# Logit rounds over pairs of head groups, split turns of the first x chunks, and finer tracking of output stores in an attention and gated-MLP block

## The chip, the core and the metric

The kernel runs on one core of a Trainium2 chip. A core has five engines that each follow their own list of instructions and meet at semaphores: TensorE (PE) for matmuls, VectorE (DVE), ScalarE (ACT), GpSimd (POOL) and SyncE (SP), which here issues every DMA. PE writes to PSUM, eight banks of 2 KB per partition; the other engines read it from there. SBUF has 128 partitions.

The metric is the device time of one execution in microseconds. Before: a median of 805.42 over three runs (805.29 to 806.07).

## The reference

Two layers over x of 2048 rows by 1024 columns, bf16. Heads: 32 of width 32; the rows are cut into 4 segments of 512.

```python
h  = x + A(layernorm(x))
h2 = h + B(layernorm(h))

# A, per head and segment s (M, z start at 0)
p     = softmax(q k^T * scale + causal mask)
a_dot = p @ v
a_mem = (phi(q) @ M) / (phi(q) @ z + 1e-6)        # phi(t) = t + 1 if t > 0 else exp(t)
o     = g * a_mem + (1 - g) * a_dot               # g = sigmoid(beta), one per head
M    += phi(k)^T v ;  z += sum(phi(k))
out   = o @ wo

# B
z1, z2 = split(gelu(x @ w_in));  z2 = layernorm(z2)
out    = (z1 * (w_sp @ z2 + b_sp)) @ w_out
```

## The kernel before

**A planner in the kernel.** Helpers (`mm`, `act`, `copy`, `tt`, `dma` and so on) only record operations, each with what it reads and writes and an estimated cost. `_Prog.op` (L91) finds the dependencies: SBUF in pieces of 32 bytes, PSUM by bank, DRAM outputs by `_where` (L78) in blocks of 128 rows. `schedule` (L148) then simulates the engines. PE keeps the order in which its operations were recorded; ACT, DVE, POOL and SP take, at each moment, the ready operation of lowest priority number, which is the recording index plus `prio`. The resulting order per engine is fixed in the program, and `link` adds the semaphore waits. So an edit of the recording order can change the order on every engine, and an engine waits at an instruction whose operands are late even if a later one could run.

**Start.** Fourteen matmuls on zeros warm up PE. `x_load` brings four chunks of 128 rows of x into XIN, halves of the weights follow on the same queue. `layernorm` takes statistics on DVE, the inverse deviation on POOL and the scaling on DVE. For segment 0, `x_turn_pe` (L548) transposes a chunk on PE, 8 transposes into one PSUM bank, and copies it to XNT (chunk 0: half by DVE and then half by ACT; chunks 1 to 3: ACT alone). Later chunks are transposed by DMA (`x_turn`). Chunk tcl+1 is turned on PE ahead of the V product of chunk tcl. Then Pq(0), Pk(0) and phi(0).

**Attention.** A step n covers one head group c = n mod 8 (4 heads) of segment s = n div 8; there are 32. For each:

- `Pq`, `Pk`: 8 matmuls of 128x512 each, copied by ACT (or DVE, for q in segment 0) into QK, which has two buffers.
- `phi`: Exp on ACT, then a minimum and one or two fused operations on DVE; K's phi is transposed by DMA into PK.
- `logits(n, r)` (L609): a round writes the transposed logits of 4 heads into PSUM banks 0 to 3, one head per bank and per row tile (`mm_row`, 32 rows each, the four run side by side). Key block j of 128 keys needs 512 - 128j query columns. Round 0 is j=0 with 512 columns, round 1 is j=1 with 384, round 2 is j=2 and 3 with 256 and 128. An exp on ACT then moves the round to E (two buffers, one for even n, one for odd), and POOL masks the diagonal blocks, one instruction of 128x512 per j. All rounds use the same four banks, so a round waits for the previous exp.
- `X(n)`: the products of E and V for query blocks 0 to 2, 24 matmuls of 33 columns.
- `MZU(n)`: the memory products (from segment 1), the E-V products of query block 3, and the update of M and z (up to segment 2). Then `combine` on DVE and POOL.

The loop over n, at L774, records: logits(n,0); Pq(n+1); X(n-1); logits(n,1); Pk(n+1); MZU(n-1); logits(n,2); phi(n+1); and then the step's fillers, V products of the next heads or segment (`v_group`) and output projections of the segment before (`wo_group`); last come loads and norms for later. Banks 4 to 7 go round for all but the logits.

**The second layer.** From 298.6 us on: w_in products with Gelu (`c1_z2`, `c1_z1`), then for each of four row blocks the w_sp products (`c2`) and the w_out products (`c3`, L935). `c2` adds a row of b_sp (BROW) into TG and multiplies into one of NY = 18 tiles Y. `c3` reads h back from the output tensor, adds, and stores column parts: two of 512 per chunk of rows, and 512, 384 and 128 for the last one. SP waits at the end for every DMA.

Of the kernel before, what the change touches and what calls it, by code (L numbers as in the profile page):

```python
# [35 lines left out]
class _Prog:  # L36
# [41 lines left out]
    def _where(self, ap):  # L78
        n = ap.tensor.name
        if n == self.psum:  # L80
            sz = mybir.dt.size(ap.dtype)
            span = ap.offset + sum(st * (c - 1) for (st, c) in [tuple(x) for x in ap.ap][1:])
            per = 2048 // sz
            off = ap.offset % (8 * per)
            last = off + span - ap.offset
            return "P", tuple(range(off // per, last // per + 1))
        if n in self.base:
            return "S", self._sbuf(ap)
        return "D", ((n, ap.offset // (128 * D)),)

# [237 lines left out]
def bass_sequential_preLN__memory_aug_infini_attn__mixer_gmlp__prompt_kernel(  # L328
# [53 lines left out]
    R_E = region(20480)  # L382
    E = [tens("e%d" % i, [128, 4, 1280], BF16, R_E + i * 10240) for i in range(2)]
    R_OT = region(16384)
# [5 lines left out]
    R_Q = cur[0]  # L390
    QK = [tens("qk%d" % i, [128, 2, L], BF16) for i in range(2)]
    EX = [tens("ex%d" % i, [128, 2, L], BF16) for i in range(1)]
# [17 lines left out]
    STATS = [tens("stats%d" % i, [128, 4, 6], F32) for i in range(4)]  # L410
    MV = [tens("mv%d" % i, [128, 2], F32) for i in range(4)]
    RS = [tens("rs%d" % i, [128, 1], F32) for i in range(4)]
    RA = [tens("ra%d" % i, [128, 12], F32) for i in range(4)]
    RM = [tens("rm%d" % i, [128, 12], F32) for i in range(4)]

    BROW = [tens("brow%d" % i, [128, L], BF16) for i in range(2)]
    TG = [tens("tg%d" % i, [128, L], BF16) for i in range(2)]
    R_END = cur[0]

    N_WARM = 14  # L420
    PS = nc.alloc_psum_tensor("ps", [128, 8, 512], F32)
    G.psum = PS.name

# [21 lines left out]

    def act(o, i, func, scale=1.0, prio=0):
        G.op(ACT, lambda e: e.activation(o, i, func, scale=scale), [i], [o],  # L447
             ((172 if inps(i) else 224) + n_of(i)) / 1.2 + 26, prio=prio, name=str(func))
# [71 lines left out]

    def layernorm(src, dst, w, prio=0):
        late[0] = prio
        k = ln_rr[0] % 4
        ln_rr[0] += 1
        nch = (w + 511) // 512
        cs = w // nch
        for ci in range(nch):
            si, so = src[:, ci * cs:(ci + 1) * cs], STATS[k][:, ci, :]
            G.op(DVE, lambda e, si=si, so=so: e.bn_stats(so, si), [si], [so], (cs + 143) / 0.96, name="bn_stats",  # L529
                 prio=late[0])  # L530
        sa, mv = STATS[k][:, 0:nch, :], MV[k][:]
        G.op(DVE, lambda e: e.bn_aggr(mv, sa), [sa], [mv], 250, name="bn_aggr", prio=late[0])  # L532
        pts1(RS[k][:], MV[k][:, 1:2], LN_EPS, ALU.add)
        ptt(RS[k][:], RS[k][:], MHALF[:], ALU.pow)
        ts(dst, src, MV[k][:, 0:1], RS[k][:], ALU.subtract, ALU.mult)
        late[0] = 0


    OFF = [0, 512, 896, 1152]
    NJ = [512, 384, 256, 128]  # L540

    def x_load(tc):
# [5 lines left out]
    def x_turn_pe(tc):  # L548
        b = bank()
        bb = b.bitcast(BF16)  # L550
        for i in range(8):
            tr(bb[:, i * 128:(i + 1) * 128], XIN[tc][:, i * 128:(i + 1) * 128])
        dst = XNT[0][:, :, tc * 128:(tc + 1) * 128]
        bv = bb.rearrange("p (c n) -> p c n", c=8)
        if tc == 0:
            copy(dst[:, 0:4, :], bv[:, 0:4, :])
            act(dst[:, 4:8, :], bv[:, 4:8, :], ACTF.Copy)
        else:
            act(dst, bv, ACTF.Copy)

# [10 lines left out]
    def Pq(n):  # L571
        s, c = divmod(n, 8)
        b = proj(WQ, s, c)
        if s == 0 and n > 0:
            copy(QK[n % 2][:, 0, :], b)
        else:
            act(QK[n % 2][:, 0, :], b, ACTF.Copy)

    def Pk(n):
        s, c = divmod(n, 8)  # L580
        act(QK[n % 2][:, 1, :], proj(WK, s, c), ACTF.Copy)

    def phi(n):
        s, c = divmod(n, 8)
        lo, hi = (0 if s >= 1 else 1), (2 if s <= 2 else 1)
        q, ex = QK[n % 2], EX[0]
        act(ex[:, lo:hi, :], q[:, lo:hi, :], ACTF.Exp, prio=40)
# [20 lines left out]

    def logits(n, r):  # L609
        q = QK[n % 2]  # L610
        js = (r,) if r < 2 else (2, 3)
        w = NJ[r] if r < 2 else 384
        for j in js:
            o0 = 0 if j < 3 else 256
            for i in range(4):
                p = slice(32 * i, 32 * i + 32)
                mm_row(PS[:, i, o0:o0 + NJ[j]], q[p, 1, j * 128:(j + 1) * 128], q[p, 0, j * 128:512], i, i == 3)
        act(E[n % 2][:, :, OFF[r]:OFF[r] + w], PS[:, 0:4, 0:w], ACTF.Exp, scale=float(SCALE))
        for j in js:
            d = E[n % 2][:, :, OFF[j]:OFF[j] + 128]  # L620
            G.op(POOL, lambda e, d=d: e.affine_select(d, d, [[0, 4], [1, 128]], ALU.is_ge, 0.0, base=0,  # L621
                                                      channel_multiplier=-1), [d], [d], 640, name="mask")

    def pv_mm(n, qb, b, col):
        s, c = divmod(n, 8)
        for i in range(4):
            for j in range(qb + 1):
                o = OFF[j] + (qb - j) * 128
                mm(b[:, col + i * 33:col + (i + 1) * 33], E[n % 2][:, i, o:o + 128], V[s % 2][:, j, 4 * c + i, 0:33],
                   j == 0, j == qb)  # L630
# [94 lines left out]
    for tcl in range(4):  # L725
        layernorm(XIN[tcl][:], XIN[tcl][:], D)
    x_turn_pe(0)
    for tcl in range(4):
        if tcl < 3:
            x_turn_pe(tcl + 1)  # L730
        v_group(0, tcl, 0)
    Pq(0)
    Pk(0)
    phi(0)

# [15 lines left out]
    plan = []  # L751
    for n in range(33):
        s, c = divmod(n, 8)
# [7 lines left out]
        if 1 <= s <= 3:  # L761
            k = (0, 0, 2, 2, 1, 1, 1, 1) if s <= 2 else (0, 0, 1, 0, 1, 1, 2, 3)
            wos = [(s - 1, g) for g in range(sum(k[:c]), sum(k[:c + 1]))]
# [10 lines left out]

    for n in range(32):
        s, c = divmod(n, 8)
        vs, wos = plan[n]
        for a, g in plan[n + 1][1]:
            if g % 2 == 0:
                h_load(4 * a + g // 2)  # L780
        logits(n, 0)
        if n + 1 < 32:
            Pq(n + 1)
        else:
            wo_group(*wos.pop(0))
        if n >= 1:
            X(n - 1)
        logits(n, 1)
        if n + 1 < 32:
            Pk(n + 1)  # L790
        else:
            wo_group(*wos.pop(0))
        if n >= 1:
            MZU(n - 1)
        logits(n, 2)
        if n + 1 < 32:
            phi(n + 1)
        for a in vs:
            v_group(*a)
        for a in wos:  # L800
            wo_group(*a)
        if n < 4:
# [15 lines left out]
        if s == 3:  # L818
# [5 lines left out]
            if c >= 6:  # L824
                win_load(c - 3)


# [76 lines left out]
    WSPT = [WSPT0, tens("wspT1", [128, 16, L], BF16, R_XNT)]  # L904
    spans[:] = [[R + 28672, R_WIN + 57344], [R_M + 2048, R_M_END]]
    NY = 18
    Y = [take("y%d" % i, [128, L], BF16) for i in range(NY)]

# [102 lines left out]
```

## Time and profile before

| what | us |
|---|---|
| median of the runs | 805.42 |
| the profiled execution, as timed | 804.33 |
| its span on the core | 802.6 |
| start, until the first logit round | 22.5 |
| segment 0 | 22.5 to 91.0 |
| segments 1 and 2 | 91.0 to 243.8 |
| segment 3 | 243.8 to 298.6 |
| second layer | 298.6 to 802.6 |
| exp of a round of 512 columns (128x2048), mean | 1.874 |
| exp of a round of 384 columns (128x1536), mean | 1.443 |
| mask of one diagonal (128x512), mean | 0.697 |

The profile is one execution, all engines recorded. Its page gives busy time by engine, the chain of work that ended last, and groups of instructions (line, engine, operation, result and operands, shapes, count; busy time and mean; idle time before it and what ended that). Other views of the same trace show instructions in order of time, or busy time by stage. Matmuls are pipelined: a row of eight starts one every 0.216 us although a single one is listed with 379 ns, so starts and not ends tell when PE was held up. TensorE's granted clock is 1.0 throughout the stages.

The landings of the first loads, from the trace's DMA events: chunk 0 at 2.95 and 3.26 us (two halves), chunk 1 at 4.94, the first half of wv at 7.95, chunk 2 at 8.63, chunk 3 at 9.33, wq at 12.33, wk at 15.35.

### The profile page before, as it was taken

The numbers are of one execution on the slowest core, as the hardware profiler recorded it, in microseconds if no ns is written. First come the engines' busy times: TensorE is split into PE (matmuls) and PEld (weight loads), VectorE is DVE, ScalarE is ACT, GpSimd is POOL, SyncE is SP. The second block draws the span as 40 slices with busy tenths as digits, with TensorE's granted clock in tenths as the row PEclk, the third lists the DMA queues.
The fourth block names the chain that finished last, engine by engine and source line by source line (L and its number), as shares of the span: only waits on it lengthen the run. The fifth ranks groups of instructions, "written<-read, shape, count | busy, mean of one in ns | idle before, by whom it ended". The sixth has DMA issues, their size and how long they took to land.

```text
span 802.6 us, 12722 instructions
## 1 busy us (share of the span) xinstructions
PE 793.7 (99%) x5372; PEld 382.7 (48%) x5372; DVE 368.6 (46%) x846; ACT 299.5 (37%) x344; POOL 154.2 (19%) x321
## 2 busy tenths in 40 slices
PE   7999999999999999999999999999999999999998
PEld 3445455555555555444445454444444444444444
DVE  5783578867766687714215041133223223322322
ACT  3888877787778863133333333100000000000000
POOL 2464445544444341100001010000000000000000
PEclk9999999999999999999999999999999999999999
DMA  9757524534233658520000026803400530011001
GB/s 309 140 129 177 114 67 87 96 84 91 69 48 95 162 107 211 170 66 1 1 1 1 3 55 129 214 1 63 128 27 1 124 93 1 0 63 49 1 7 47
DMA packets 128458, 64.81 MB, mean 81 GB/s; under 512 B 95504, under 2 KB 120336, under 8 KB 128400
## 3 DMA queue, kind: packets, MB, share of 16 engines
q1 hardware_dynamic: 128400, 63.99, 33.2%
q8 instruction: 42, 0.69, 0.4%
q14 instruction: 16, 0.13, 0.1%
HBM read 32.51 MB, written 8.39 MB: 51 GB/s over the span
## 4 chain that ended last, share of the span: by engine, by line
PE 96%; DMA 1%; ACT 1%; DVE 1%; SPq 0%; issue 0%
PE ps L435 93%; PE ps L440 3%; DMA xin<-in_A_x_dram 1%; DVE stats L529 0%; ACT e L447 0%; SPq L490 0%; ACT ex L447 0%; ACT qk L447 0%; PE ps L444 0%; DVE qk L459 0%; DVE xin L463 0%; DVE hx L469 0%; DVE mv L532 0%
## 5 line engine op out<-in xcount | busy, mean ns | idle before, releaser
L435 PE MATMUL ps<-wspT,z 128*128 128x512 bf16 x896 | 194.0, 379 | 0.0
L447 ACT ACTIVATE e<-ps 128x1536 bf16<-128x1536 f32 (+1 forms) x96 | 152.3, 1587 | 38.9 <-PE ps L440 38.9
L435 PEld LDWEIGHTS ps<-wspT,z 128*128 128x128 bf16 x896 | 87.7, 98 | 105.7
L447 ACT ACTIVATE z<-ps 128x512 bf16<-128x512 f32 x120 | 68.2, 569 | 140.0 <-PE ps L435 140.0
L469 DVE TENSOR_TENSOR tg<-ps,brow 128x512 bf16<-128x512 f32 x56 | 38.7, 692 | 152.6 <-PE ps L435 122.7
L621 POOL TENSOR_SCALAR_AFFINE_SELECT e<-e 128x512 bf16<-128x512 bf16 x128 | 88.3, 697 | 98.7 <-ACT e L447 98.4
L435 PE MATMUL ps<-win,hnT 128*128 128x512 bf16 (+1 forms) x512 | 97.8, 352 | 0.0
L435 PE MATMUL ps<-wout,y 128*128 128x512 bf16 (+2 forms) x462 | 97.4, 373 | 0.0
L435 PE MATMUL ps<-hnT,win 128*128 128x512 bf16 x448 | 97.3, 379 | 0.0
L529 DVE BATCH_NORM_STATS2 stats<-z 128x6 f32<-128x448 bf16 x64 | 39.9, 624 | 95.1 <-ACT z L447 93.5
L469 DVE TENSOR_TENSOR hx<-hx,ps 128x512 bf16<-128x512 bf16 (+1 forms) x65 | 43.6, 677 | 79.4 <-PE ps L435 77.0
L435 PEld LDWEIGHTS ps<-win,hnT 128*128 128x128 bf16 x512 | 50.0, 98 | 47.8 <-ACT e L447 0.2
L435 PEld LDWEIGHTS ps<-wout,y 128*128 128x128 bf16 x462 | 44.7, 98 | 52.3
L435 PEld LDWEIGHTS ps<-hnT,win 128*128 128x128 bf16 x448 | 43.9, 98 | 52.1
L435 PE MATMUL ps<-xnT,wk 128*128 128x512 bf16 x256 | 60.8, 380 | 0.0
L435 PE MATMUL ps<-xnT,wq 128*128 128x512 bf16 x256 | 60.8, 380 | 0.0
L435 PE MATMUL ps<-wv,xnT 128*128 128x512 bf16 x256 | 59.9, 380 | 0.1
L435 PE MATMUL ps<-wo,oT 128*128 128x512 bf16 x256 | 58.8, 379 | 0.0
L483 POOL TENSOR_SCALAR rs<-mv 128x1 f32<-128x1 f32 x48 | 10.7, 223 | 185.0 <-DVE mv L532 184.5
L435 PEld LDWEIGHTS ps<-v,e 128*128 128x128 bf16 x1280 | 40.5, 96 | 9.2
L435 PE MATMUL ps<-v,e 128*128 128x33 bf16 x1280 | 42.0, 177 | 0.0
L447 ACT ACTIVATE qk<-ps 128x512 bf16<-128x512 f32 x57 | 34.1, 598 | 10.9 <-PE ps L435 10.4
(58 smaller groups left out, 565.6 us busy)
## 6 DMA issues: line engine op xcount, KB each, us to landing
win<-in_B_w_in_dram SPq DMA_DIRECT2D x6, 1024.0 KB, 5.5
hx<-in_A_x_dram SPq DMA_DIRECT2D x16, 256.0 KB, 3.0
out_dram<-hx SPq DMA_DIRECT2D x16, 256.0 KB, 2.4
hx<-out_dram SPq DMA_DIRECT2D x16, 256.0 KB, 2.6
out_dram<-hx SPq DMA_DIRECT2D x31, 128.0 KB, 1.8
xin<-in_A_x_dram SPq DMA_DIRECT2D x15, 256.0 KB, 6.0
wout<-in_B_w_out_dram SPq DMA_DIRECT2D x2, 1792.0 KB, 10.2
wv<-in_A_wv_dram SPq DMA_DIRECT2D x2, 1024.0 KB, 9.1
```

The costliest lines, as they stand in the source:

```text
L435: G.op(PE, lambda e: e.matmul(o, lhsT, rhs, start=start, stop=stop), [lhsT, rhs], [o], max(n / 2.4 + 2.6, 25.0), lag=166, name="mm " + lhs ...
L440: G.op(PE, lambda e: e.matmul(o, lhsT, rhs, start=True, stop=True, tile_position=(32 * i, 0)), [lhsT, rhs], [o], n / 2.4 if last else 3.5, ...
L447: G.op(ACT, lambda e: e.activation(o, i, func, scale=scale), [i], [o], ((172 if inps(i) else 224) + n_of(i)) / 1.2 + 26, prio=prio, name=s ...
L469: G.op(DVE, lambda e: e.tensor_tensor(o, a, b, op), [a, b], [o], vcost(o, [a, b], fast), name="tt", prio=late[0])
L483: G.op(POOL, lambda e: e.tensor_single_scalar(o, i, s, op), [i], [o], 220 if n_of(o) < 8 else 220 + 2.5 * n_of(o), name="pts1", prio=late[0])
L529: G.op(DVE, lambda e, si=si, so=so: e.bn_stats(so, si), [si], [so], (cs + 143) / 0.96, name="bn_stats", prio=late[0])
L621: G.op(POOL, lambda e, d=d: e.affine_select(d, d, [[0, 4], [1, 128]], ALU.is_ge, 0.0, base=0, channel_multiplier=-1), [d], [d], 640, name= ...
```

## The change

Everything is computed as before; order, buffers and tracking change.

1. **Rounds.** The loop runs over 16 pairs (a, b) of head groups with five rounds of 512 columns: (a, j=0); (a, j=1) with (a, j=3); (a, j=2) with (b, j=2); (b, j=0); (b, j=1) with (b, j=3). E becomes one tensor with a region for each kind of round, and an exp writes the second and third kind in blocks of 256 columns. A mask instruction covers 4 diagonal blocks for j=0 and 8 for the others. QK gets a third buffer, since three groups are alive. The pair's fillers are dealt to five slots.
2. **Start.** A turn uses two banks, 4 transposes each; the first is copied by DVE (ahead of other work, `late` = -200), the second by ACT. The turn of the next chunk stands after five of the eight V matmuls. Pk(0) is made in two parts, K columns 0 to 127 first.
3. **Stores.** A DRAM access is tracked by row block and by 128-column block.
4. **Small.** Y has 14 tiles; BROW and TG move into memory that the first layer leaves; MV is wider; `layernorm` can scale on ACT, which no call uses (`BYACT` is all 0).

```diff
-        return "D", ((n, ap.offset // (128 * D)),)
+        w = list(ap.ap)[-1][1]
+        c0 = ap.offset % D
+        return "D", tuple((n, ap.offset // (128 * D), c) for c in range(c0 // 128, (c0 + w + 127) // 128))
...
-    E = [tens("e%d" % i, [128, 4, 1280], BF16, R_E + i * 10240) for i in range(2)]
+    E = tens("e", [128, 10240], BF16, R_E)
...
-    QK = [tens("qk%d" % i, [128, 2, L], BF16) for i in range(2)]
+    QK = [tens("qk%d" % i, [128, 2, L], BF16) for i in range(3)]
...
+    AT = [5, 5, 5, 9]
...
     def x_turn_pe(tc):
-        b = bank()
-        bb = b.bitcast(BF16)
-        for i in range(8):
-            tr(bb[:, i * 128:(i + 1) * 128], XIN[tc][:, i * 128:(i + 1) * 128])
         dst = XNT[0][:, :, tc * 128:(tc + 1) * 128]
-        bv = bb.rearrange("p (c n) -> p c n", c=8)
-        if tc == 0:
-            copy(dst[:, 0:4, :], bv[:, 0:4, :])
-            act(dst[:, 4:8, :], bv[:, 4:8, :], ACTF.Copy)
-        else:
-            act(dst, bv, ACTF.Copy)
+        for h in range(2):
+            bb = bank().bitcast(BF16)
+            for i in range(4):
+                c = 4 * h + i
+                tr(bb[:, i * 128:(i + 1) * 128], XIN[tc][:, c * 128:(c + 1) * 128])
+            bv = bb[:, 0:512].rearrange("p (c n) -> p c n", c=4)
+            if h == 0:
+                late[0] = -200
+                copy(dst[:, 0:4, :], bv)
+                late[0] = 0
+            else:
+                act(dst[:, 4:8, :], bv, ACTF.Copy)
...
+    def logits(parts):
+        for n, j, col in parts:
+            q = QK[n % 3]
             for i in range(4):
                 p = slice(32 * i, 32 * i + 32)
+                mm_row(PS[:, i, col:col + NJ[j]], q[p, 1, j * 128:(j + 1) * 128], q[p, 0, j * 128:512], i, i == 3)
+        n, j, _ = parts[0]
+        m, src = n % 2, PS[:, 0:4, :]
...
+        elif j == 2:
+            src = PS[:, 0:4, :].rearrange("p i (b q) -> p b i q", b=2)
+            o = E[:, ER3[0]:ER3[0] + 2048].rearrange("p (b i q) -> p b i q", b=2, i=4)
...
+        act(o, src, ACTF.Exp, scale=float(SCALE))
+        pat = [[0, 4 if j == 0 else 8], [1, 128]]
+        G.op(POOL, lambda e: e.affine_select(d, d, pat, ALU.is_ge, 0.0, base=0, channel_multiplier=-1), [d], [d],
+             1270 if j else 640, name="mask")
...
     for tcl in range(4):
-        if tcl < 3:
-            x_turn_pe(tcl + 1)
-        v_group(0, tcl, 0)
+        b = bank()
+        for i in range(8):
+            if i == AT[tcl] and tcl < 3:
+                x_turn_pe(tcl + 1)
+            mm(b[:], XNT[0][:, i, tcl * 128:(tcl + 1) * 128], WV[:, i, 0:512], i == 0, i == 7)
+        act(V[0][:, tcl, 0:16, 0:32], b.rearrange("p (h d) -> p h d", d=32), ACTF.Copy)
     Pq(0)
-    Pk(0)
+    for lo, hi in ((0, 128), (128, 512)):
+        b = bank()
+        for i in range(8):
+            mm(b[:, 0:hi - lo], WK[:, i, 0:128], XNT[0][:, i, lo:hi], i == 0, i == 7)
+        act(QK[0][:, 1, lo:hi], b[:, 0:hi - lo], ACTF.Copy)
     phi(0)
...
+    for pair in range(16):
+        a, b = 2 * pair, 2 * pair + 1
+        fill = [(v_group, x) for n in (a, b) for x in plan[n][0]] + [(wo_group, x) for n in (a, b) for x in plan[n][1]]
...
+        order = (2, 4, 0, 4, 1) if pair < 15 else (2, 2, 3, 4)
...
+        logits([(a, 0, 0)])
+        Pq(b)
+        filler(0)
+        if a:
+            X(a - 1)
+        logits([(a, 1, 128), (a, 3, 0)])
+        Pk(b)
+        if a:
+            MZU(a - 1)
+        phi(b)
+        filler(1)
+        chores(a)
+        logits([(a, 2, 0), (b, 2, 256)])
+        if pair < 15:
+            Pq(b + 1)
+        filler(2)
+        logits([(b, 0, 0)])
+        if pair < 15:
+            Pk(b + 1)
+            phi(b + 1)
+        X(a)
+        filler(3)
+        logits([(b, 1, 128), (b, 3, 0)])
+        MZU(a)
+        filler(4)
+        chores(b)
...
-    NY = 18
+    BROW = [take("brow%d" % i, [128, L], BF16) for i in range(2)]
+    TG = [take("tg%d" % i, [128, L], BF16) for i in range(2)]
+    NY = 14
```

`chores(n)` holds the loads and norms that the old loop had at its end. In the built order, DVE's list at the start reads: statistics of chunks 0 and 1, scaling of chunk 0, copy of turn 0, the first half of chunk 2's statistics, scaling of chunk 1, the second half, copy of turn 1, the rest of chunk 2's and chunk 3's statistics, scaling of chunk 2, copy of turn 2, scaling of chunk 3, copy of turn 3. In segment 3, ACT's list has the Exp of phi(b) ahead of the exp of (a, j=1 and 3).

## The prediction

> **What bounds the kernel now.** I read the page's head first, then the chain of waits, then a table of stages, then the order in time where those point.
>
> ```profile
> span 802.6 us, 12722 instructions
> PE 793.7 (99%) x5372; PEld 382.7 (48%) x5372; DVE 368.6 (46%) x846; ACT 299.5 (37%) x344; POOL 154.2 (19%) x321
> ```
>
> TensorE (PE) is busy 99% of the span. So time can only leave in three ways: PE has less to do, its few idle places go, or the two ends shrink. The table of stages (PE busy after the length) says where idle places are: 0.7 us in the first segment, none in segments two and three, nearly none later.
>
> ```profile
> 22.50:91.00 68.50, 67.80 (x714) 33.78 (x715) 43.81 (x104) 59.15 (x57) 35.78 (x76) 1.00 0.73 156
> 91.00:243.80 152.80, 152.80 (x1539) 78.17 (x1537) 113.61 (x314) 117.30 (x113) 72.10 (x134) 1.00 0.37 76
> ```
>
> Next the chain of waits over one head group of segment 0 (start, length, what). L440 is a logit round, L435 all other matmuls.
>
> ```profile
> 59.85 0.34 PE ps L440 x4
> 60.19 2.43 PE ps L435 x32
> 62.62 0.27 PE ps L440 x4
> 62.89 2.47 PE ps L435 x28
> 65.36 0.28 PE ps L440 x8
> 65.64 1.83 PE ps L435 x8
> ```
>
> Eight plain 128x512 matmuls take 1.73 us in the chain where nothing else intervenes, 0.216 each. Behind a round and before the next they take 1.83: 0.10 us is lost on the way into a round. A round itself is 0.34 for 512 columns, 0.27 for 384, 0.28 for 256 and 128. At 0.213 us for 512 columns (four row tiles run side by side) that is 0.10 to 0.12 over its columns: the way out. A round therefore costs **0.20 us** besides its columns, and two parts inside one round (the x8 row) cost no second one.
>
> **1. Rounds.** Before: 3 rounds per group, 96. After: 5 per pair, 80. The columns stay (1280 per group). Exactly: old pair 2 x (0.34+0.27+0.28+3 x 0.10) = 2.38; new pair five rounds of 512 columns, 5 x (0.34+0.10) = 2.20. From the start times of single matmuls, less rounded, the difference is 0.199. 16 pairs x 0.199 = **-3.2 us**. Here a rule of the Trainium skill weighs in (page "TensorEngine Tiling (Array Packing)", Key Properties): changing the tiling mode drains TensorE. A 128x512 matmul has a mean of 379 ns but steps by 216, so a full drain would be 163 ns each way, and 16 x 0.326 = 5.2 us. The row shows 0.10 each way; I take the row.
>
> **2. The wait that pairing adds.** The round (a2,b2) needs K of b, which Pk(b) has just made; before, a group's K was two rounds old when first read. PE issues in order, so everything behind that round waits too. The nearest rows are these:
>
> ```profile
> 62.55 0.34 PE L440 MATMUL ps<-qk 32*128 32x384 bf16 x4
> 62.82 1.90 PE L435 MATMUL ps<-xnT,wk 128*128 128x512 bf16 x8
> 62.95 1.45 ACT L447 ACTIVATE e<-ps 128x1536 bf16<-128x1536 f32 x1 [0.69 <-PE ps L440]
> 64.56 0.56 PE L435 MATMUL ps<-v,e 128*128 128x33 bf16 x16
> 64.76 0.60 ACT L447 ACTIVATE qk<-ps 128x512 bf16<-128x512 f32 x1 [0.37 <-PE ps L435]
> 65.30 0.34 PE L440 MATMUL ps<-qk 32*128 32x256 bf16 x8
> ```
>
> Count from Pk's start (62.82): the copy of K starts at +1.94, ends at +2.54, and PE can start 0.05 later (the step from ACT's end to PE seen at 22.45 to 22.50): +2.59. PE arrives after Pk and MZU, +2.47 (65.30 less 62.82, rounded): stall **0.12**. In segments 1 and 2 MZU holds four memory products more (0.22), PE arrives at +2.69: no stall, 0.1 of slack. In segment 3 there is no V-PK product and PE arrives at +2.45: 0.14. ACT must be free at +1.94. The exp of (a1,a3) now covers 2048 columns, 1.87 us busy, 1.75 until the next can start; it begins 0.46 after its round, so ACT is free at +1.88. In segment 3, though, the built order puts the Exp of phi(b), 0.63 us, ahead of that exp. It delays it by 0.2 to 0.35 where no filler stands before X, and K with it. I sum 0.45, 0.14, 0.32, 0.32 for its four pairs: 1.23. Segment 0, pairs 1 to 3: 0.36. Pair 0 has no MZU in between at all: 2.59 against 1.73+0.10, so 0.76. Together **+2.35 us**. The other rounds keep 2.5 us and more from the previous exp, as now. V, Wo, X and MZU are moved but not changed. The PSUM bank that is nearest to a wait is X(a)'s, in pairs with two fillers at the end: its last DVE read ends 2.4 us after (b1,b3), PE wants it at 2.9.
>
> The skill has a rule against widening rounds (same page, PSUM Bottleneck): once tiling has sped up TensorE, emptying PSUM may become the limit. All exps sit on ACT. But it has five of 1.87 = 9.35 us per pair, where it had 2 x (1.87+1.45+1.43) = 9.50, and the stage row shows 59.15 of 68.50. By the rule ACT sets segment 0 and its four pairs' 0.8 us of saving are lost; by the row only the stalls above remain. I follow the row.
>
> The three exps in 256-column blocks, and the masks over 1024 columns, have no row. Exp: 1.87 at the least (same elements); at most 2.12, past which nothing of the gain is left (rival C). I take 1.87, as 1536 and 2048 columns (1443 and 1874 ns) differ by columns alone. Mask: between 1.23 (two in succession at 59.81) and 2 x 0.697 = 1.39. X(b) needs it some 3.65 us after (b1,b3) and comes at 4.85, so it is hidden at either end.
>
> **3. Old stalls.** Segment 0's 0.7 us are 0.27 (the second round of group 0), 0.20 near 45 us (V waiting for a late DVE read of its bank) and 0.44 at 83.07 (a round behind a late exp); a PE row is drawn longer than its step, so 0.91 of lost steps shows as 0.70. The last two have Exp of phi or a full DVE ahead of what PE needs; in the new order the exp goes ahead of phi there. **-0.64**. The first stays (0.28).
>
> **4. The start.** PE's first logit is at 22.50.
>
> ```profile
> 8.55 0.62 PE L444 MATMUL ps<-ident,xin 128*128 128x128 bf16 x8 [1.05 <-DVE xin L463]
> 8.65 1.42 DVE L529 BATCH_NORM_STATS2 stats<-xin 128x6 f32<-128x512 bf16 x2 [0.16 <-DMA xin<-in_A_x_dram]
> 22.50 0.39 PE L440 MATMUL ps<-qk 32*128 32x512 bf16 x4 [0.69 <-ACT qk L447]
> ```
>
> After: turn 0 is copied by DVE and ACT side by side (two banks), so V0 can start when its weights land, 8.0 (the landing is in the trace's DMA events). Its first five matmuls end at 9.08. But DVE's new order has the first statistics of chunk 2 before the scaling of chunk 1, and chunk 2 lands only at 8.65: scaling 9.38 to 9.93, turn 1 at 9.98 instead of 8.55. V0 ends 11.08; five of V1 until 12.16; turn 2 waits for DVE until 12.86; V1 ends 13.96; five of V2, turn 3 at 15.04; V2 16.14; V3 17.87. Pq starts at 17.87, was 18.19: -0.32. The filled gaps are mostly given back to DVE's late scaling. Then Pk in two parts: 8 x 56 + 8 x 163 ns = 1.75 for 1.73, but the first round needs K's first 128 columns alone, so its wait behind Pk (0.69 in the row and the way in) goes: Pq to the round takes 3.58, took 4.31: -0.73. Start **-1.05**. If chunk 2 lands early enough for DVE, another 1 us goes; if DVE slips further, the 0.32 is lost.
>
> **5. The tail.** SP issues the third last-row store at 800.64, though its data are ready at 799.46:
>
> ```profile
> 799.01 1.96 SPq L490 DMA_DIRECT2D out_dram<-hx  x2
> 799.17 0.29 DVE L469 TENSOR_TENSOR hx<-hx,ps 128x128 bf16<-128x128 bf16 x1 [0.23 <-PE ps L435]
> ```
>
> It waited for the store of the neighbouring columns to land. With tracking per column block it goes at 799.50: **-1.14**, all on the end. The same waits at earlier stores stand on SP with nothing late behind them: no gain. What is late next is the same store's own flight.
>
> **6. At nothing.** 14 instead of 18 y tiles: y of the next block is written after 16 matmuls (3.5 us) that follow the last reader; without them a wait of 0.7 per tile. Moved BROW and TG: that memory's last user ended some 200 us earlier (it served the attention part). Third QK buffer: it only removes waits. SP's queue: loads of h are issued a pair earlier and x transposes keep their order; transposes of PK get half a pair more slack.
>
> **Sum**: -3.2+2.35-0.64-1.05-1.14 = -3.7. The profiled execution took 804.33 (span 802.6 and 1.73 around it), so 800.7 by its own time; the median of the runs stands 1.09 above it: 805.42 - 3.7 = **801.8**.
>
> **The rivals.**
> A (0.68), the forecast: 801.8, own range 800.4 to 803.6.
> B (0.14): K of b is never late, by a shorter copy or a slower MZU; the 2.35 vanish: 799.4. For it: the stalls are of 0.1 us, near rounding. Against: pair 0 has no cover at all.
> C (0.11): the blocked exps take 0.25 more. K then comes 0.25 later in every pair (0.15 beyond the slack in segments 1 and 2): 0.25 x 8 + 0.15 x 8 = 3.2, and the time is 805.0, no change. Against: ACT's rows follow columns.
> D (0.07), slower: something of 0.6 us (a V copy) stands before the exp of (a1,a3) in every pair, K is 0.6 late: 1.36 in pair 0, 3 x 0.72, 8 x 0.5, 0.9 x 4 = 11.1 of stalls against 6.0 of gains: 810.5. It decides from 0.4 us per pair (6.0/16). The built order shows such a piece in segment 3 only.
>
> **How the numbers follow.** A measurement of this kernel can tell 0.2% (1.6 us) from no change. Faster by more: A and B, 0.82; within: C, 0.11; slower: D, 0.07. The range 799.2 to 804.4 takes in A, B's centre and a smaller C; it leaves out D and the rest of C.
>
> **What would show it.** 80 rounds in the page's groups; no idle PE in segments 1 and 2; PE waiting for the ACT copy of qk before 8 matmuls of 256 columns, 0.76 once and 0.1 to 0.45 seven times; first logit near 21.45; the last store issued right behind DVE. Wrong if PE waits for exp or mask in every pair, if exps in blocks are over 1.9 us, or if turn 1 runs before 9.9.

## The result, and the profile after

| | before | after |
|---|---|---|
| median of the runs | 805.52 (805.29 to 806.07, 4 runs) | 799.87 (799.55 to 801.09, 4 runs) |
| ratio | | 0.9932, 95% interval 0.9914 to 0.9949 |
| profiled execution, as timed | 804.33 | 799.55 |
| its span | 802.6 | 797.8 |
| first logit round starts | 22.50 | 21.40 |
| first logit round to last matmul | 776.41 | 773.43 |
| last matmul to end of span | 3.70 | 2.99 |
| logit rounds | 96 | 80 |

The forecast was 801.8, of which the sum on the profile was -3.7 us. The profile shows -4.8: -1.10 at the start, -2.98 between, -0.71 at the end. (The medians moved by 5.65, because the profiled execution of before lies 1.1 under its median and that of after only 0.3.) These three stretches are used for every run below, because their sum is the span and because each part of the change acts in one of them. The end is taken with the span to three decimals (802.609 before, 797.819 after), so it differs by a few hundredths from the 3.69 and 2.97 that some expectations quote.

The head of the page of after, and the lines of exp and mask from the groups with shapes kept apart (count, busy us and mean ns; idle time before):

```profile
span 797.8 us, 12571 instructions
PE 783.6 (98%) x5284; PEld 382.1 (48%) x5380; DVE 369.5 (46%) x849; ACT 293.0 (37%) x329; POOL 140.3 (18%) x273
...
L450 ACT ACTIVATE e<-ps 128x2048 bf16<-128x2048 f32 x80 | 149.7, 1872 | 40.2 <-PE ps L441 40.2
L653 POOL TENSOR_SCALAR_AFFINE_SELECT e<-e 128x1024 bf16<-128x1024 bf16 x48 | 55.4, 1154 | 48.7 <-ACT e L450 48.4
```

PE's busy time seems to fall by 10 us. Up to half of that is an artefact: 5284 matmuls are listed beside 5380 weight loads, so 96 matmul records are missing here and none in before (5372 and 5372). One is missing in every 50 to 84 matmuls, all along the program, and half of them lie in the second layer. Each leaves a hole of about 0.05 us in a row of matmuls (two steps of 0.216 less 379 ns), an estimated 5 us in all. Where the missing one is the first behind a round (17 cases), the row shows as "x7" and starts about 0.22 late. So idle time was read from start times, with a missing record counted as a matmul.

The exps are what the forecast took: 1872 ns in 256-column blocks too, 1874 before. The mask over 1024 columns takes 1.154 us in the mean, below the lower of the two bounds given (1.23), and is less than two over 512 columns (0.635 each in after). The mean mixes 32 masks of about 1.09 us with some of up to 1.53.

**The wait that pairing adds.** The order in time of after in pair 0, where nothing stands between Pk(b) and the round that needs its K:

```profile
24.15 1.90 PE L436 MATMUL ps<-xnT,wk 128*128 128x512 bf16 x8
...
26.09 0.60 ACT L450 ACTIVATE qk<-ps 128x512 bf16<-128x512 f32 x1
...
26.20 0.29 PE L441 MATMUL ps<-qk 32*128 32x256 bf16 x4 [0.15 <-ACT e L450]
...
26.74 0.29 PE L441 MATMUL ps<-qk 32*128 32x256 bf16 x4 [0.25 <-ACT qk L450]
```

The round is drawn as two rows of four. The first, a's 256 columns, starts at 26.20, when the exp before has let go of the banks; the second, b's, starts when the K copy is done (it runs from 26.09 to 26.69). Without any wait the first would start at 25.98 (Pk starts at 24.15, takes 1.73, and 0.10 is the way in) and the second 0.11 behind it. The stall is 0.22 + 0.43 = 0.65 us. The first part ends with the exp and not with K, but K alone would have held b's columns for the same 0.65. The same place in pair 3 of segment 0, where MZU stands between:

```profile
71.25 0.60 ACT L450 ACTIVATE qk<-ps 128x512 bf16<-128x512 f32 x1
...
71.78 0.41 PE L441 MATMUL ps<-qk 32*128 32x256 bf16 x8
```

All eight matmuls of the round form one row: K is ready at 71.85, 0.07 after the round began, and b's columns come 0.12 after it began. No stall. Segments 1 and 2 have none either; segment 3 has two of 0.165 (in the rounds at 271.5 and 286.7). The first of them is drawn longer than the row above by its stall:

```profile
271.50 0.57 PE L441 MATMUL ps<-qk 32*128 32x256 bf16 x8
```

One stall of another kind is new: X waits 0.13 for a mask, until 53.40.

**Sum of the middle stretch.** From start times, a round of 512 columns lasts 0.327 (one part) or 0.330 (two parts) until the next plain matmul; the old rounds of 384 and of 256 + 128 lasted 0.274 and 0.276; the way in is 0.096 behind 512-column matmuls in both. So rounds give 32 x (0.327 + 0.274 + 0.276) + 96 x 0.096 = 37.28 before, and 32 x 0.327 + 48 x 0.330 + 80 x 0.096 = 33.98 after: -3.3. New stalls are 0.65 + 0.33 + 0.13 = 1.11. Of the old ones, those that ended at 50.34 (0.20) and 83.07 (0.43) are gone, and the one of group 0 stays. -3.3 + 1.11 - 0.63 = -2.8, against -2.98 measured; 0.2 us lie below what this count resolves. Nothing of it comes from the second layer: from the last product of E and V to the last matmul, before and after take 491.44 us each.

**The end.** Before, SP issued the third last-row store late; now (order in time, after):

```profile
794.89 0.85 SPq L493 DMA_DIRECT2D out_dram<-hx  x2
795.09 0.29 DVE L472 TENSOR_TENSOR hx<-hx,ps 128x128 bf16<-128x128 bf16 x1 [0.23 <-PE ps L436]
```

The first row holds the last two issues on SP; the second of them follows DVE's addition above it at once. The last store leaves SP 0.57 us after the last matmul (1.73 before), as forecast. But from its landing at 796.90 to the end of the span is 0.9 us, where before it was 0.5 (from 802.09). The semaphore events on SP show why. SP closes the program with a row of waits, one for each store semaphore, about 0.063 us apart. Before, the last store's wait stood near the end of the row. In after it stands ahead of seven others, which are satisfied by then and still take their turn from 796.92 to 797.36.

### The profile page after: what moved, and what is told of

The parts are those of the page before. It is cut to its first block, busy times and chain, and to the rows that moved or that the text cites. A ratio compares the mean times of both kernels' runs of the same rounds, so it can differ in the third digit from the quotient of the medians.

```text
span 797.8 us, 12571 instructions
## 1 busy us (share of the span) xinstructions
PE 783.6 (98%) x5284; PEld 382.1 (48%) x5380; DVE 369.5 (46%) x849; ACT 293.0 (37%) x329; POOL 140.3 (18%) x273
## 4 chain that ended last, share of the span: by engine, by line
PE 96%; issue 1%; DMA 1%; DVE 1%; ACT 1%; SPq 0%
PE ps L436 93%; PE ps L441 3%; DMA xin<-in_A_x_dram 1%; ACT e L450 0%; DVE stats L532 0%; SPq L493 0%; PE ps L445 0%; ACT qk L450 0%; DVE hx L472 0%; DVE xin L466 0%; ACT ex L450 0%; DVE xnT L462 0%; DVE rm L479 0%; DVE mv L535 0%; DVE rm L469 0%
## 5 line engine op out<-in xcount | busy, mean ns | idle before, releaser
L450 ACT ACTIVATE e<-ps 128x2048 bf16<-128x2048 f32 x80 | 149.7, 1872 | 40.2 <-PE ps L441 40.2
L472 DVE TENSOR_TENSOR tg<-ps,brow 128x512 bf16<-128x512 f32 x56 | 38.7, 691 | 152.8 <-PE ps L436 122.9
L653 POOL TENSOR_SCALAR_AFFINE_SELECT e<-e 128x1024 bf16<-128x1024 bf16 (+1 forms) x80 | 75.7, 946 | 106.9 <-ACT e L450 106.6
L436 PE MATMUL ps<-xnT,wk 128*128 128x512 bf16 (+2 forms) x248 | 57.2, 373 | 2.5 <-issue 1.3
L436 PE MATMUL ps<-wv,xnT 128*128 128x512 bf16 x232 | 56.8, 379 | 1.9 <-DMA wv<-in_A_wv_dram 0.6
L436 PEld LDWEIGHTS ps<-wo,oT 128*128 128x128 bf16 x256 | 24.7, 98 | 28.5 <-DVE ta L472 0.2
```

The source lines that it names most:

```text
L436: G.op(PE, lambda e: e.matmul(o, lhsT, rhs, start=start, stop=stop), [lhsT, rhs], [o], max(n / 2.4 + 2.6, 25.0), lag=166, name="mm " + lhs ...
L450: G.op(ACT, lambda e: e.activation(o, i, func, scale=scale, **kw), r, [o], ((172 if inps(i) else 224) + n_of(i)) / 1.2 + 26, prio=prio, na ...
L472: G.op(DVE, lambda e: e.tensor_tensor(o, a, b, op), [a, b], [o], vcost(o, [a, b], fast), name="tt", prio=late[0])
L653: G.op(POOL, lambda e: e.affine_select(d, d, pat, ALU.is_ge, 0.0, base=0, channel_multiplier=-1), [d], [d], 1270 if j else 640, name="mask")
```

## The experiments

One profiled execution per run, split as above (us). V0 is the first V product; it starts when the first half of wv has landed or, with the old turns, behind turn 1. The kernels e3, e4, e6 and e7 ran once each, so what they show is read from their traces and not from a median.

| run | V0 starts | V0 to first logit | first logit to last matmul | to the end | span |
|---|---|---|---|---|---|
| before | 9.01 | 13.49 | 776.41 | 3.70 | 802.6 |
| after | 8.30 | 13.10 | 773.43 | 2.99 | 797.8 |
| e1 rounds only | 9.10 | 13.45 | 773.29 | 3.72 | 799.6 |
| e2 start only | 9.07 | 13.16 | 777.49 | 3.70 | 803.4 |
| e3 b first | 8.07 | 13.11 | 774.21 | 2.98 | 798.4 |
| e4 split round | 8.03 | 13.09 | 777.41 | 2.97 | 801.5 |
| e5 stores only | 8.85 | 14.26 | 776.21 | 2.98 | 802.3 |
| e6 closing waits | 8.21 | 13.11 | 773.28 | 2.47 | 797.1 |
| e7 scaling first | 7.86 | 12.82 | 773.57 | 2.99 | 797.2 |
| e8 after again | 8.65 | 13.10 | 773.29 | 2.98 | 798.0 |
| e9 combined | 8.23 | 12.66 | 774.62 | 2.47 | 798.0 |
| e10 all scalings first | 8.51 | 13.94 | 774.03 | 2.49 | 799.0 |
| e11 scaling 1 and waits | 8.49 | 12.87 | 773.59 | 2.47 | 797.4 |

### One part alone: rounds, start, stores

**e1** is the changed kernel with the old start and the old tracking of stores.

```diff
-    for lo, hi in ((0, 128), (128, 512)):
...
+    Pk(0)
...
-        return "D", tuple((n, ap.offset // (128 * D), c) for c in range(c0 // 128, (c0 + w + 127) // 128))
+        return "D", ((n, ap.offset // (128 * D)),)
```

> The changed kernel with its start and its store tracking as before: only the paired rounds are left. Switch theory (a round costs 0.20 us besides its columns, 16 fewer): -3.2, the old stalls of segment 0 gone -0.64, two new kinds of K wait +0.75 (0.42 in pair 0, 0.33 in segment 3), so a span 3.1 us under before's 802.6, 799.5; first logit at 22.5 as before. Rival (the rounds bring little, start and tail the rest of the 4.8): span within 1.5 us of 802.6.

Measured: 801.53 (801.28 to 802.05), 0.9957 of before (0.994 to 0.9973). The middle stretch has all of the gain of after, and the two ends are those of before. The waits in the paired round are the same. So the paired rounds alone are worth about 3.1 us on the profile, stalls included.

**e2** is before with the new turns, V order and K in two parts.

```diff
-            act(dst, bv, ACTF.Copy)
...
+                copy(dst[:, 0:4, :], bv)
...
+                act(dst[:, 4:8, :], bv, ACTF.Copy)
...
-    Pk(0)
+    for lo, hi in ((0, 128), (128, 512)):
```

> Before, with the new start alone (turns in halves inside the V products, K of group 0 in two parts). Theory: first logit at 21.4 instead of 22.50, so 1.1 us off the span (801.5), of which 0.35 by the turns (Pq at 17.85 instead of 18.19) and 0.73 by the K parts; all of it stays, since PE is the bound behind it. Rival (an earlier start is lost again in segment 0, where loads of the next segment arrive as late as before): first logit at 21.4, span 802.6.

Measured: 804.63 (804.09 to 805.19), 0.9996 (0.9987 to 1.0005): no change that the runs can tell, and the interval (-1.0 to +0.4 us) just leaves out the 1.1 of the theory. The start was only 0.26 earlier, since chunk 2 landed 1 us later in this execution (9.67). What little it gained was more than lost in the middle, 777.49 against 776.41. The order in time of e2 shows where:

```profile
48.04 0.69 DVE L530 BATCH_NORM_STATS2 stats<-xin 128x6 f32<-128x512 bf16 x1 [4.20 <-DMA xin<-in_A_x_dram]
...
50.44 0.67 DVE L460 CAST qk<-ps 128x512 bf16<-128x512 f32 x1
...
51.17 1.68 PE L436 MATMUL ps<-wv,xnT 128*128 128x512 bf16 x7 [1.23 <-DVE qk L460]
```

DVE stood 4.20 us for an x chunk of the next segment. The Q copy queued behind that chunk's statistics, and PE's next V product waited 1.23 us for the bank that this copy empties (0.20 at this place before). The profiled execution was the slowest of the twelve (805.19; median 804.63), so how much of this loss the others have is not known. In the paired loop the middle stretch is the same with the old start (e1, 773.29) and with the new one (after 773.43, e8 773.29), so in these executions a start that is early stays early.

**e5** is before with the tracking per column block.

```diff
-        return "D", ((n, ap.offset // (128 * D)),)
+        return "D", tuple((n, ap.offset // (128 * D), c) for c in range(c0 // 128, (c0 + w + 127) // 128))
```

> Before, with the tracking of output stores per column block alone. Before spends 3.69 us from the start of its last matmul to the end of the span, the changed kernel 2.97. Theory (the last store no longer waits, -1.14 to -1.16, but SP's closing waits, about 0.065 us each, then stand behind the last landing, up to +0.45): 2.5 to 3.0 us here, so 0.7 to 1.2 off the span, all of it behind the last matmul; first logit and stalls as before. Rival (other store waits on SP had delayed reads of h, so that matmuls gain as well): last matmul earlier than before's 798.9 by over 0.3 with the same start.

Measured: 804.43 over 20 runs, 0.9989 (0.9982 to 0.9995), so -0.9 us (-0.4 to -1.45). The end is 2.98, as in after (2.99), and the row of waits on SP again has seven behind the one that matters. The start of this execution was 0.6 late by its loads (chunk 2's statistics begin at 9.27, at 8.65 before), which hides the gain in its span. The store edit is worth 0.72 on the profile, not 1.14; the interval of the runs holds both, so it is the trace that tells them apart.

### Why the added wait is smaller than forecast

**e3** swaps the two parts of the shared round.

```diff
-        logits([(a, 2, 0), (b, 2, 256)])
+        logits([(b, 2, 256), (a, 2, 0)])
```

> The changed kernel with the parts of the round (a,2)+(b,2) issued in the order b, a. Theory (K of b is as late as forecast, but a's 256 columns, 0.11 us, run before it is read and cover that much): the waits for K of b come back at 0.11 us more each where it is the last to arrive: 0.53 in pair 0, about 0.1 in three pairs of segment 0 and 0.1 to 0.3 in four of segment 3; +0.6 to +0.9 in all. Rival (the copy of K is simply earlier than forecast): no change, waits as in the changed kernel.

Measured: 800.09 in one run; the middle stretch is 0.78 longer than after. The shared round of pair 0 in e3, in order of time:

```profile
23.93 1.90 PE L436 MATMUL ps<-xnT,wk 128*128 128x512 bf16 x8
...
25.87 0.60 ACT L450 ACTIVATE qk<-ps 128x512 bf16<-128x512 f32 x1
...
26.52 0.40 PE L441 MATMUL ps<-qk 32*128 32x256 bf16 x8 [0.69 <-ACT qk L450]
```

The stall here is 0.76, the forecast's number for the whole round, and four of 0.12 appear where after has none (until 41.6, 56.7, 71.9 and 88.7; the last is in the first pair of segment 1, whose MZU still belongs to segment 0). The K copy comes just as late, 1.94 after Pk's start. So it is the order in the round: a's 256 columns need nothing of b and take 0.11 us, and they cover 0.11 of each wait. With b first the K waits are 0.76 + 4 x 0.12 + 0.05 + 0.12 + 0.28 + 0.28 = 1.97; with a first they are 0.65 + 0.33 = 0.98. Of this difference of 0.99, the stretch shows 0.78, because after has the mask wait of 0.13, which e3 has not, and five of its pairs still lose 0.01 to 0.02 each inside the round.

### What a round costs

**e4** splits one of the five rounds of each pair, by putting the first products of MZU between the two parts of (b1, b3).

```diff
+            if between and j == 3:
+                between()
-        logits([(b, 1, 128), (b, 3, 0)])
+        logits([(b, 1, 128), (b, 3, 0)], lambda: MZ_first(a))
```

> The changed kernel with the first products of MZU(a) moved between the parts (b,1) and (b,3) of the last round of each pair: no work more, 16 changes into and out of row tiling more. Row theory (0.10 in and 0.10 out): +3.2 us on the span. Rule theory (a full drain of 0.163 each way): +5.2. Rival (a change of mode costs nothing, the saving of the change had another cause): 0.

Measured: 803.25 in one run; the middle stretch is 3.98 longer. One mask wait of 0.54 until 38.7 (where after has 0.13 at 53) is part of it. That leaves 3.6 for 16 more rounds, 0.22 each. The split pieces show in the order in time:

```profile
63.97 0.34 PE L441 MATMUL ps<-qk 32*128 32x384 bf16 x4
64.24 0.57 PE L436 MATMUL ps<-v,e 128*128 128x33 bf16 x16
64.74 0.23 PE L441 MATMUL ps<-qk 32*128 32x128 bf16 x4
64.91 0.41 PE L436 MATMUL ps<-v,pk 128*128 128x132 bf16 x4
```

From starts, the pieces last 0.273 and 0.167 where the whole lasted 0.330, and a second way in costs 0.096: 0.21 per round. The forecast's 0.20 from the rows stands. The Trainium skill ("TensorEngine Tiling (Array Packing)", Key Properties) says that changing the tiling mode drains TensorE, and gives no time for it. The estimate of 0.163 us each way that the forecast weighed beside it would have made 0.33 per round and 5.2 us; the trace shows less.

### The end, and the start once more

**e6** puts SP's closing waits into the order in which the stores land.

```diff
-        self.dma_ends = [(dsem[j], cnt[j]) for j in range(npool)]
+        landed = {o.sem: o.t1 for o in sorted((o for o in ops if o.dma), key=lambda o: o.t1)}
+        by_landing = sorted(range(npool), key=lambda j: landed[j])
...
+        self.dma_ends = [(dsem[j], cnt[j]) for j in ends]
```

> The changed kernel with SP's closing waits in the order in which the DMAs land, the last store last. Theory (seven further waits of about 0.065 us stand behind the last landing in the changed kernel): 0.4 us less from the last matmul's start to the end, 2.55 instead of 2.97. Rival (the end is set by the landing and a fixed close): 2.97.

Measured: 798.8 in one run. Last matmul to end is 2.47 against 2.99; SP's last wait now ends with the landing (796.66), and the program ends 0.4 after it. That is the whole of the missing 0.43 (1.14 less 0.71), and 0.1 more, since before had one wait behind the decisive one as well.

**e7** holds DVE's first statistics of chunk 2 behind the scaling of chunk 1.

```diff
+        k0 = len(G.ops)
+        if tcl == 2:
+            scale1 = k0 - 1
         layernorm(XIN[tcl][:], XIN[tcl][:], D, by_act=BYACT[tcl])
+        if tcl == 2:
+            G.ops[k0].deps.add(scale1)
```

> The changed kernel with the scaling of chunk 1 put ahead of chunk 2's statistics on DVE. Theory (DVE's whole list behind chunk 2's landing sets the start, so the stall only moves): turn 1 follows five V matmuls at once (0.67 of stall gone), the stall at turn 2 grows by as much less 0.2; first logit 0.2 earlier relative to the landing of chunk 2 (21.40 and 8.83 in the changed kernel). Rival (the order of DVE alone held the start): stall at turn 2 as now, first logit 0.7 to 0.9 earlier.

Measured: 798.96 in one run. The start of after, and then of e7, in order of time:

```profile
8.85 0.69 DVE L532 BATCH_NORM_STATS2 stats<-xin 128x6 f32<-128x512 bf16 x1 [0.95 <-DMA xin<-in_A_x_dram]
9.46 0.53 DVE L466 TENSOR_SCALAR xin<-xin,mv,rs 128x1024 bf16<-128x1024 bf16 x1
...
10.05 0.62 PE L445 MATMUL ps<-ident,xin 128*128 128x128 bf16 x8 [0.51 <-DVE xin L466]
```

```profile
7.65 0.55 DVE L466 TENSOR_SCALAR xin<-xin,mv,rs 128x1024 bf16<-128x1024 bf16 x1 [0.20 <-POOL rs L482]
...
8.94 0.61 PE L445 MATMUL ps<-ident,xin 128*128 128x128 bf16 x8
...
12.11 0.62 PE L445 MATMUL ps<-ident,xin 128*128 128x128 bf16 x8 [0.60 <-DVE xin L466]
```

In after, scaling 1 follows the first statistics of chunk 2, which had waited for its landing until 8.85; in e7 it runs before. Turn 1 then comes 1.08 after V0's start (7.86) instead of 1.75. But turn 2 still waits for DVE (0.60): its work on chunk 2 begins with the landing, whatever was done before. From V0's start to the first logit only 0.28 of the 0.67 is left. Turn 1 was late, as forecast, but most of what it lost was lost again at turn 2.

**e8** is the changed kernel again, without any edit.

> The changed kernel once more, as partner of the next run on the same chip: about 799.9.

Measured: 799.53 (799.48 to 799.8, 5 runs), 0.9921 (0.9908 to 0.9935). The result repeats; the mask wait at 53 does not appear.

**e9** joins e7 and e6 and adds two edits: the copies of turns 1 to 3 all on ACT, and in segment 3 the Exp of phi(b) behind the exp of (a1, a3).

```diff
-            if h == 0:
+            if h == 0 and tc > 0:
+                act(dst[:, 0:4, :], bv, ACTF.Copy)
...
+        if s == 3 and last_exp[0] is not None:
+            G.ops[-1].deps.add(last_exp[0])
```

> The changed kernel with scaling 1 ahead of chunk 2's statistics, copies of turns 1 to 3 on ACT alone, the Exp of phi in segment 3 behind the exp of (a,1)+(a,3), and the closing waits in order of landing. Theory: start 0.3 us less (DVE loses three copies of 0.42 behind chunk 2's landing), the two stalls of 0.16 in segment 3 gone, 0.4 at the end: 1.0 us under the changed kernel, about 798.9. Rival (ACT's copies of turns or a later phi hold PE instead): no change or slower, with PE waiting for ACT in turns 1 to 3 or in MZU of segment 3.

Measured: 799.74 (799.15 to 801.53), 0.9927 (0.9914 to 0.9939): nothing over e8, taken on the same chip. Each edit did its part where it was aimed: 12.66 to the first logit, 2.47 at the end, and the stalls in segment 3 fell from 0.33 to about 0.02. But 1.11 went in one place (order in time, e9):

```profile
53.26 1.09 POOL L668 TENSOR_SCALAR_AFFINE_SELECT e<-e 128x1024 bf16<-128x1024 bf16 x1
...
54.41 0.64 PE L444 MATMUL ps<-v,e 128*128 128x33 bf16 x19 [0.95 <-POOL e L668]
```

The exp that this mask follows ended at 50.6. POOL came to the mask at 53.26, because two small multiplications ahead of it (at 52.03 and 53.11) had waited 0.50 and 0.88 us for DVE. DVE was behind with its work; at 38.36 it had stood 3.17 us for an x chunk (that this is why it was late at 52 is likely, but not shown). Another 0.46 is a K product at 45.88, which the profile puts down to the second half of wk landing late. Here the mask is late by its place in POOL's queue, not by its length.

**e10** is after with e6's waits, and e7's edit for chunk 3 as well; **e11** is after with e6's and e7's edits and nothing else.

```diff
-        if tcl == 2:
+        if tcl >= 2:
```

> Edits: the changed kernel, with DVE's first statistics of chunks 2 and 3 held behind the scaling of the chunk before, and SP's closing waits in the order in which the stores land. Theory (DVE's order sets the turns, 0.28 us were gained by chunk 2 alone between V0's start and the first logit, 13.10 to 12.82; closing waits give 0.42): chunk 3 brings turn 2 forward by up to another 0.65, of which 0.3 to 0.5 should reach the first logit (12.3 to 12.5 after V0's start), and the end comes 2.55 after the last matmul: profile about 798.5, against 799.55. Rival (what is early at the start waits again in segment 0, as in the run of all edits together, where X waited 1.1 us at 53 us for a mask behind POOL and DVE, with DVE held 3.17 us by an x chunk): from the first logit to the last matmul it takes 0.5 to 1.5 us more than 773.4, and the time is 799 to 800, no better than the changed kernel.

> Edits: the changed kernel, with DVE's first statistics of chunk 2 held behind the scaling of chunk 1, and SP's closing waits in the order in which the stores land; nothing else of the run of all edits together. Theory (both gains are on the path and independent): first logit 12.82 after V0's start, first logit to last matmul 773.4 to 773.6, end 2.55 after the last matmul: 0.28 + 0.42 = 0.7 us less than the changed kernel, profile about 798.9, median about 0.7 below the changed kernel's. Rival (the start gain is lost in segment 0): only the 0.42 remain.

Measured: e10 801.02 (800.69 to 802.88), 0.9945 (0.9932 to 0.9957), slower than e11 on the same chip in every run (e11's highest is 799.73). The theory fell at the start itself: turn 2 came at +4.10 after V0 (after: +4.53), but now chunk 3 was late, since its statistics waited for scaling 2. In order of time:

```profile
15.45 0.55 DVE L474 TENSOR_SCALAR xin<-xin,mv,rs 128x1024 bf16<-128x1024 bf16 x1 [1.00 <-POOL rs L490]
...
16.05 0.62 PE L453 MATMUL ps<-ident,xin 128*128 128x128 bf16 x8 [1.09 <-DVE xin L474]
```

DVE idled 1.00 each time while POOL made the scale (two operations); before, the next chunk's statistics filled that time. Turn 3 waited 1.09, and the mask wait (until 55.05) grew to 0.72. The rival was right that there is nothing to win, partly for another reason than its own.

e11: 799.59 (798.78 to 799.73), 0.9919 (0.9905 to 0.9932). Both parts are there (V0 to first logit -0.23, end -0.52), while V0 began 0.19 later with its weights and the mask wait at 53 came to 0.28. Beside e8's 0.9921 it is no difference that the runs can tell. No version was shown to beat the changed kernel.

## Why the prediction was right, and which step failed

**Rounds, -3.2**: right. -3.3 from the starts of single matmuls; e4 prices one round at 0.21, where 0.20 was taken.

**The wait that pairing adds, +2.35**: this step failed in its size. It measured 0.98 (0.65 in pair 0, 0.33 in segment 3). The arrival of K was forecast well: the copy began 1.94 after Pk's start, took 0.60, and PE followed 0.05 later. The error is the sentence "PE issues in order, so everything behind that round waits too", from which each wait was counted from the start of the round. PE does issue in order, but the round's first four matmuls are a's, and they stand ahead of the waiting ones. Their 0.11 us came off every wait, which left nothing of the three of 0.12. e3 shows this directly: 1.97 with b first. That explains 0.99 of the 1.37. The remaining 0.4 was mainly the first pair of segment 3: 0.45 was taken for the Exp of phi ahead of the exp, and with b first it is 0.05. The MZU of that pair still belongs to segment 2, so PE arrives 2.70 after Pk's start (after) where 2.45 was counted; the rest of that pair's error is open.

**Old stalls, -0.64**: right in size, 0.63 went and the one of group 0 stayed. In part that is luck: the V wait of 0.20, which the forecast put near 45 us, ended at 50.34, and e5, which has the old loop too, does not show it.

**Start, -1.05**: right, -1.10, with turns at 10.05, 12.83 and 15.01 where 9.98, 12.86 and 15.04 were worked out. Its larger part is firm: from Pq's start to the first round takes 3.57 in after and in e8 (3.58 forecast), and 4.31 before. That the turns fit to 0.07 is luck as well, since they follow loads that move: with this start the first round came between 21.12 and 21.75 (after, e3, e4, e6, e8). The remark "if chunk 2 lands early enough for DVE, another 1 us goes" stays open: e7 removes the wait at turn 1 by the order on DVE, not by an earlier landing, and wins 0.28. In the old loop (e2) the runs show no gain from the same start.

**Tail, -1.14**: this step failed in its size too. The store did leave that much earlier, but -0.71 reached the end. The forecast followed the store to its landing and put what changes behind it at nothing. There, SP's closing waits made 0.9 us of 0.5; e6 gets 0.52 back.

**At nothing**: exps in blocks, right to 2 ns. The mask was called hidden at either end of its price, and still X waited for one: 0.13 in after, 0.27 in e7, 0.28 in e11, more in e4, e10 and e9 (0.54, 0.72, 1.11), and nothing in e1, e3, e6 and e8. The margin was worked out from the mask's duration and left out what stands ahead of it on POOL. In after the exp ends at 50.6, and POOL reaches the mask only at 52.25. Ahead of it, it waits for DVE twice:

```profile
50.60 0.21 POOL L482 TENSOR_TENSOR ra<-ra,g 128x12 f32<-128x12 f32 x1 [0.50 <-DVE ra L479]
51.68 0.20 POOL L482 TENSOR_TENSOR ra<-ra,g 128x4 f32<-128x4 f32 x1 [0.88 <-DVE ra L479]
51.86 0.44 POOL L482 TENSOR_TENSOR mz<-msum,gmask 128x132 bf16<-128x132 f32 x1
```

In e8, the same program, the mask starts 1.47 behind the exp instead of 1.64, and X does not wait. In e7 and e11 it starts 1.52 and 1.53 behind the exp, but is listed with 1.36 instead of 1.09 us; what lengthens it is open.

Put together: the sum was 1.1 us too small on the profile (-3.7 against -4.8). The K wait gives 1.4 of that, the tail takes 0.4 back, and the rest is within 0.2. The forecast time was 1.9 off: the other 0.8 comes from adding 1.09 for the distance between the profiled execution and the median, which was 0.3 in after. The outcome lies between the first case (801.8) and rival B (799.4). That it is near B in time is luck of these executions: on the profile -4.8 stands about midway between -3.7 and B's -6.0. Nor is B's mechanism the one at work: K is as late as forecast, and it is covered. Rivals C and D are refuted by the exp's 1872 ns and by the absence of stalls in segments 1 and 2. The Trainium skill ("TensorEngine Tiling (Array Packing)", PSUM Bottleneck) says only that copying out of PSUM may become the limit once tiling has sped up TensorE. That ACT would then set segment 0 was the forecast's reading, and it did not come about: behind pair 0, PE waited there only the 0.13 for a mask and some hundredths in rounds.

## What to carry to other kernels

A wait counts from the instruction that needs the data, not from the group it belongs to: ask what of the same group can be issued first, and put it first. When a start or an engine's queue is made faster, look for the next thing on that queue that does not come earlier with it (here the x loads that DVE waits for), because the gain can end there. Follow the last store past its landing; the order of the closing waits was worth 0.4 to 0.5 us.

## What was not expected of the hardware

- Each satisfied wait in SP's closing row takes 0.063 us (after, 796.92 to 797.36), so seven of them behind the decisive one cost 0.44.
- In after, 32 of the 48 masks over 1024 columns are listed with about 1.09 us, and one over 512 takes 0.635. From these a fixed part of about 0.18 each is estimated (2 x 0.635 - 1.09).
- The landing of the first loads moves from run to run: chunk 2 landed at 8.36 (e7) to 9.67 (e2) in these executions, and V0 of the kernels with the new start, which waits for wv, began between 7.86 and 9.07. This is about as large as the effects of the start edits, so they were compared from V0's start.
- The way out of a round costs the same for 128 columns as for 512. Rounds of 512 and of 384 columns last 0.327 and 0.274, so 128 columns are 0.053 and 512 are 0.213. What is left is 0.114 both for the piece of 128 columns in e4 (0.167 less 0.053) and for the round of 512 (0.327 less 0.213).
